# Two gaps in SBUF ahead of the experts' operands in an attention and expert-layer kernel

## The chip, the cores and the metric

The kernel runs on one core of a Trainium2 chip. The metric is the device time of one execution in microseconds (us), lower is better. TensorE is called PE, VectorE DVE, ScalarE ACT, GpSimd POOL and SyncE SP; PEld is PE's loading of the stationary operand. SBUF addresses are bytes within a partition.

## The reference

Attention over 8 batches of 8 heads: 512 local positions, each of which sees its neighbours within 32 positions and 32 global ones, and 32 global positions that see all. Its output, 4352 rows of 512 numbers, goes through an expert layer: each row goes to the one of 8 experts whose embedding is nearest in direction, and comes back weighted with the gate.

```python
xn = x / (norm(x) + 1e-6); en = emb / (norm(emb) + 1e-6)
logits = xn @ en.T / tau
e = argmax(logits); gate = softmax(logits)[e]
out[row] = gate * (relu(x[row] @ w1[e]) @ w2[e])     # w1[e]: 512 x 1024, w2[e]: 1024 x 512
```

All inputs and the output are float32.

## The kernel before

The first stage computes attention, four steps to a batch, and routes each row: its gate and number are put behind its 512 values, and an indirect DMA scatters it into a table in DRAM with a region for each expert. Two blocks of 128 rows of the first expert are computed early, in plain float32 matmuls (`early_block`, lines 157 to 184), from the raw weights in the stage tiles stg0 and stg1. Their pieces (1024 numbers and a gap of two) begin 4104 bytes apart.

The second stage runs `item(w, prev)` 36 times, in an order written out by hand. An item is 128 rows of one expert. For float32 accuracy at the matmul's single-pass type float32r, each operand is split in two: a high part, rounded to float32r, and a low part, what the rounding left. WH and WL hold the parts of the weights, four slots of 4096 numbers each: `w_part` makes them from stg, a half of an expert during each item, with a cast on ACT (L1172) and a subtraction on DVE or POOL (L1174). `x_parts` transposes the item's rows (L1154) and splits them into xH and xL (L1156, L1157); `h_parts` does that for the hidden layer (L1201, L1203, L1204) into hH and hL. `up` and `down` then make three matmuls for each product: high by high (L1178) and low weights (L1179) in `high`, and the low rows by high weights (L1183) in `low`. In all of them the part of x or h is the stationary operand, 128x128, and 512 columns of WH or WL are the moving one. From the third item on the slot of WH and WL comes from a register; in the first two it is fixed.

DMAs bring the next item's raw weights (2 MB, SP's queue) and the rows of the item after the next. The result goes out by an indirect DMA on POOL (L142).

Where a tile lies follows from the order in which the tiles are made: pools follow each other, and each tile takes its size rounded up to 32 bytes. The pools of the second stage, wp (WH, WL), xi (xr0 to xr2), xh (xH0, xH1, xL0, xL1), hb (h), ht (hL, hH) and obp (ob), lie over those of the attention stage, which are dead by then, and a tile waits for the tiles under it. In the program before, WH begins at byte 55,904 and WL at 121,440, both 96 past a multiple of 512; xH0 at 193,216 and, with steps of 2048 and 4096, the other parts, h, hL and hH begin 192 past one. The stage tiles stg0 and stg1 begin at 22,368 and 38,784, which is 352 and 384 past one.

Of the kernel before, what the change touches and what calls it, by code (L numbers as in the profile page):

```python
# [12 lines left out]
F32 = mybir.dt.float32  # L13
# [20 lines left out]
P = 128  # L34
# [65 lines left out]
def tile_kernel(ctx: ExitStack, tc: tile.TileContext, qk, va, emb, tau, wraw, cst, out):  # L100
# [30 lines left out]
    def cols(st, lo, hi):  # L131

        r = lo // WRUN
        return st[:, r, lo - r * WRUN : hi - r * WRUN]
# [886 lines left out]
    wp = ctx.enter_context(tc.tile_pool(name="wp", bufs=1, reuse_waits="tile"))  # L1021
    xi = ctx.enter_context(tc.tile_pool(name="xi", bufs=1, reuse_waits="tile"))
    xh = ctx.enter_context(tc.tile_pool(name="xh", bufs=1, reuse_waits="tile"))
# [6 lines left out]
    ps_1 = ctx.enter_context(tc.tile_pool(name="ps_1", bufs=3, space=PSUM, reuse_waits="tile"))  # L1030


    WH = wp.tile([P, 4, 4096], F32R, name="WH")
    WL = wp.tile([P, 4, 4096], F32R, name="WL")
    WH2 = WH.rearrange("p (s h) n -> p s (h n)", s=2)
    WL2 = WL.rearrange("p (s h) n -> p s (h n)", s=2)

    xrs = [xi.tile([P, ROW], F32, name=f"xr{i}") for i in range(3)]
    xHs = [xh.tile([P, 4, P], F32R, name=f"xH{i}") for i in range(2)]
    xLs = [xh.tile([P, 4, P], F32R, name=f"xL{i}") for i in range(2)]  # L1040

# [78 lines left out]
    def first_parts(hf, c):  # L1120

        cs = slice(c * 1024, (c + 1) * 1024)
        src = cols(st0[hf], cs.start, cs.stop)
        nc.scalar.copy(WH[:, hf, cs], src)
        eng = nc.gpsimd if hf == 1 and c < 2 else nc.vector
        eng.tensor_tensor(WL[:, hf, cs], src, WH[:, hf, cs], ALU.subtract)  # L1126

# [31 lines left out]
    def item(w, prev):  # L1159
# [9 lines left out]
        def w_part(c):  # L1169
            cs = slice(c * 512, (c + 1) * 512)  # L1170
            s3 = cols(st, cs.start, cs.stop).unsqueeze(1)
            made.append(nc.scalar.copy(WH[:, ds(ra, 1), cs], s3))  # L1172
            eng, r = (nc.vector, rv) if c % 2 == 1 else (nc.gpsimd, rg)
            made.append(eng.tensor_tensor(WL[:, ds(r, 1), cs], s3, WH[:, ds(r, 1), cs], ALU.subtract))  # L1174

# [204 lines left out]
```

## Time and profile before

| | us |
|---|---|
| median of 3 runs | 739.73 (738.18 to 742.41) |
| the profiled execution's own time | 740.73 |
| its span, first to last instruction | 738.9 |
| PE busy | 683.4 (92%) |
| ACT busy | 458.7 (62%) |
| DVE busy | 424.2 (57%) |

Busy matmuls overlap: the length of a matmul in the profile reaches beyond the start of the next, so its price in a stream is the step from start to start. The time outside the span is 740.73 − 738.9 = 1.8 us.

### The profile page before, as it was taken

How to read it: one execution, taken by the hardware profiler on the slowest of the kernel's cores; microseconds unless marked ns; L12 is line 12 of the kernel's file. 1: busy time of each engine (PE TensorE's matmuls, PEld its weight loads, DVE VectorE, ACT ScalarE, POOL GpSimd, SP SyncE). 2: the span in 40 equal slices, each digit the busy share in tenths (PEclk: the TensorE clock that was granted, in tenths of full speed). 3: DMA queues.
4: the chain of work that ended last, by engine and by line, in shares of the span. 5: the costliest groups of instructions: out<-in, count | busy, mean ns of one | idle time of the engine just before them, and what ended most of it. 6: DMA issues, size and time to landing. Idle time of an engine off the chain costs nothing.

```text
span 738.9 us, 23354 instructions
## 1 busy us (share of the span) xinstructions
PE 683.4 (92%) x7867; PEld 535.5 (72%) x7869; DVE 424.2 (57%) x1449; ACT 458.7 (62%) x956; POOL 274.7 (37%) x318
## 2 busy tenths in 40 slices
PE   8888878877878989999999999999999999999995
PEld 4666667655666547888888888888888888888884
DVE  2777677888677575545454555555454545554543
ACT  3776766857657265656565656566666656666653
POOL 2011122221122444544454535444444444454542
PEclk9999999999899999999999999999999999999998
DMA  9988878978997266647474656566565656565744
GB/s 276 340 234 247 274 215 270 289 212 284 281 289 219 96 219 245 247 168 257 160 255 171 231 193 225 204 202 225 192 222 180 245 177 242 174 237 178 258 155 148
DMA packets 66301, 165.14 MB, mean 223 GB/s; under 512 B 6516, under 2 KB 14580, under 8 KB 66176
## 3 DMA queue, kind: packets, MB, share of 16 engines
q1 hardware_dynamic: 60416, 145.67, 59.4%
q0 software_dynamic: 5760, 17.87, 6.8%
q8 instruction: 71, 1.16, 0.7%
q14 instruction: 54, 0.44, 0.2%
HBM read 142.49 MB, written 22.07 MB: 223 GB/s over the span
## 4 chain that ended last, share of the span: by engine, by line
PE 85%; issue 6%; DVE 4%; DMA 2%; ACT 1%; SPq 0%; POOL 0%; DVEq 0%; POOLq 0%
PE g L1183 18%; PE g L1178 18%; PE g L1179 18%; PE po L515 5%; PE pt L492 4%; PE hps L1201 4%; PE s_ps L445 4%; PE pt L632 2%; PE xps L1154 2%; DMA raw<-in_qk_dram 2%; PE po L334 2%; PE pt L600 1%; PE pt L552 1%; DVE WL L1126 1%; PE s_ps L434 1%
## 5 line engine op out<-in xcount | busy, mean ns | idle before, releaser
L1174 DVE TENSOR_TENSOR WL<-stg,WH 128x512 f32 (+1 forms) x144 | 149.6, 1039 | 125.3 <-ACT WH L1172 125.3
L1174 POOL TENSOR_TENSOR WL<-stg,WH 128x512 f32 (+1 forms) x144 | 174.1, 1209 | 90.3 <-ACT WH L1172 89.4
L1172 ACT CAST WH<-stg 128x512 f32 (+1 forms) x288 | 177.7, 619 | 4.5 <-ACT ob L140 0.5
L1178 PE MATMUL g<-WH,hH 128*128 (+1 forms) x288 | 120.0, 417 | 0.0
L1178 PE MATMUL g<-WH,xH 128*128 (+1 forms) x288 | 117.3, 407 | 0.0
L1183 PE MATMUL g<-WH,xL 128*128 (+1 forms) x288 | 114.2, 397 | 1.7 <-DVE ob L141 1.7
L1179 PE MATMUL g<-WL,xH 128*128 (+1 forms) x288 | 114.1, 396 | 0.0
L1179 PE MATMUL g<-WL,hH 128*128 (+1 forms) x288 | 113.6, 394 | 0.0
L142 POOL DMA_INDIRECT out_dram<-ob x37 | 37.3, 1009 | 154.9 <-ACT ob L140 140.8
L485 ACT ACTIVATE pb<-pb,nm 128x128 f32<-128x128 f32 x256 | 80.0, 395 | 12.3 <-DVE nm L468 12.3
L1204 DVE TENSOR_TENSOR hL<-hps,hH 128x512 fp32r<-128x512 f32 x72 | 49.8, 691 | 62.7 <-ACT hH L1203 62.7
L1183 PE MATMUL g<-WH,hL 128*128 (+1 forms) x288 | 84.6, 395 | 0.0
L1183 PEld LDWEIGHTS g<-WH,xL 128*128 128x128 f32 x288 | 54.0, 188 | 15.1 <-DVE ob L141 2.1
L1195 ACT ACTIVATE h<-g 128x512 f32<-128x512 f32 x72 | 42.8, 594 | 35.3 <-PE g L1183 35.3
L1183 PEld LDWEIGHTS g<-WH,hL 128*128 128x128 f32 x288 | 54.4, 189 | 13.1
L1178 PEld LDWEIGHTS g<-WH,xH 128*128 128x128 f32 x288 | 54.3, 189 | 11.8 <-issue 0.2
L1179 PEld LDWEIGHTS g<-WL,xH 128*128 128x128 f32 x288 | 54.4, 189 | 11.6 <-issue 0.2
L140 ACT ACTIVATE ob<-g,xr 128x512 f32<-128x512 f32 x36 | 24.8, 688 | 60.9 <-PE g L1183 60.9
L772 POOL DMA_INDIRECT xs<-xt,si x32 | 32.1, 1003 | 81.7 <-PE s_ps L445 30.4
L1179 PEld LDWEIGHTS g<-WL,hH 128*128 128x128 f32 x288 | 54.4, 189 | 9.8
L1178 PEld LDWEIGHTS g<-WH,hH 128*128 128x128 f32 x288 | 54.2, 188 | 9.7
L1203 ACT CAST hH<-hps 128x512 fp32r<-128x512 f32 x72 | 42.1, 584 | 26.4 <-PE hps L1201 26.3
(200 smaller groups left out, 991.4 us busy)
## 6 DMA issues: line engine op xcount, KB each, us to landing
stg<-in_wraw_dram SPq DMA_DIRECT2D x36, 2048.0 KB
vt<-in_va_dram SPq DMA_DIRECT2D x94, 260.0 KB
raw<-in_qk_dram SPq DMA_DIRECT2D x56, 304.0 KB
xr<-xs SPq DMA_DIRECT2D x38, 257.0 KB
stg<-in_wraw_dram SPq DMA_DIRECT2D x16, 256.0 KB
vt<-in_va_dram SPq DMA_DIRECT2D x30, 130.0 KB
xs<-fill SPq DMA_DIRECT2D x12, 257.0 KB
stg<-in_wraw_dram SPq DMA_DIRECT2D x4, 512.0 KB
```

Source lines behind the costliest of these rows:

```text
L142: nc.gpsimd.indirect_dma_start(out=out[:, :], out_offset=bass.IndirectOffsetOnAxis(ap=ob[:, DM : DM + 1].bitcast(U32), axis=0), in_=ob[:, ...
L485: nc.scalar.activation(pb[:, cs], pb[:, cs], AF.Exp, bias=nm[:, n : n + 1], scale=-1.0)
L515: ins = nc.tensor.matmul(po[32 * k : 32 * k + 32, grp, j * VH : (j + 1) * VH], pT[:, col(s, k, j) : col(s, k, j) + 32], vals(b, _window(4 ...
L772: ins = nc.gpsimd.indirect_dma_start(out=xs[:, :], out_offset=bass.IndirectOffsetOnAxis(ap=st["si"][:, t : t + 1], axis=0), in_=get(t), in ...
L1172: made.append(nc.scalar.copy(WH[:, ds(ra, 1), cs], s3))
L1174: made.append(eng.tensor_tensor(WL[:, ds(r, 1), cs], s3, WH[:, ds(r, 1), cs], ALU.subtract))
L1178: reads.append(nc.tensor.matmul(o.unsqueeze(1), a, WH2[:, ds(rp, 1), sl], start=first, stop=False))
L1179: reads.append(nc.tensor.matmul(o.unsqueeze(1), a, WL2[:, ds(rp, 1), sl], start=False, stop=False))
L1183: reads.append(nc.tensor.matmul(o.unsqueeze(1), a, WH2[:, ds(rp, 1), sl], start=False, stop=last))
L1195: nc.scalar.activation(h[:, nh * 512 : (nh + 1) * 512], g, AF.Relu)
L1203: nc.scalar.copy(hv, hp_)
L1204: nc.vector.tensor_tensor(hL[:, nh * 4 : nh * 4 + 4, :].rearrange("p c n -> p (c n)"), hp_, hv, ALU.subtract)
```

## The change

Two tiles of 104 float32 numbers, 416 bytes, are made and never used: one ahead of WH, one ahead of xH0. All that follows in the second stage's pools moves by 416 bytes, and behind the second gap by 832. WH, WL, xH, xL, h, hL and hH then begin on multiples of 512 bytes (56,320, 121,856, 194,048 and so on); the row tiles xr move from 96, 128 and 160 past a multiple to 0, 32 and 64. The attention stage's tiles and the stage tiles stay where they are.

```diff
@@ -1030,12 +1030,14 @@
     ps_1 = ctx.enter_context(tc.tile_pool(name="ps_1", bufs=3, space=PSUM, reuse_waits="tile"))
 
 
+    wp.tile([P, 104], F32, name="gap0")
     WH = wp.tile([P, 4, 4096], F32R, name="WH")
     WL = wp.tile([P, 4, 4096], F32R, name="WL")
     WH2 = WH.rearrange("p (s h) n -> p s (h n)", s=2)
     WL2 = WL.rearrange("p (s h) n -> p s (h n)", s=2)
 
     xrs = [xi.tile([P, ROW], F32, name=f"xr{i}") for i in range(3)]
+    xh.tile([P, 104], F32, name="gap1")
     xHs = [xh.tile([P, 4, P], F32R, name=f"xH{i}") for i in range(2)]
     xLs = [xh.tile([P, 4, P], F32R, name=f"xL{i}") for i in range(2)]
```

## Rows read from the trace of the kernel before

**Rows 1.** The page: busy us (share of the span) and instructions.
```profile
span 738.9 us, 23354 instructions
PE 683.4 (92%) x7867; PEld 535.5 (72%) x7869; DVE 424.2 (57%) x1449; ACT 458.7 (62%) x956; POOL 274.7 (37%) x318
```

**Rows 2.** The stretch of the items, with its columns.
```profile
core 0: us, PE busy (x) PEld busy (x) DVE busy (x) ACT busy (x) POOL busy (x), PEclk, DMA share, GB/s
...
279.50:729.70 450.20, 449.86 (x2156) 366.75 (x2157) 223.59 (x290) 282.04 (x501) 210.40 (x180) 1.00 0.60 211
```

**Rows 3.** The chain that ended last, by engine, from the page.
```profile
PE 85%; issue 6%; DVE 4%; DMA 2%; ACT 1%; SPq 0%; POOL 0%; DVEq 0%; POOLq 0%
```

**Rows 4.** The same chain in order of time: each item's last four matmuls.
```profile
291.22 0.94 PE g L1183 x4
303.75 0.94 PE g L1183 x4
...
716.98 0.94 PE g L1183 x4
```

**Rows 5.** The page's costliest groups: busy us, mean ns of one | idle before.
```profile
L1178 PE MATMUL g<-WH,hH 128*128 (+1 forms) x288 | 120.0, 417 | 0.0
...
L1183 PE MATMUL g<-WH,xL 128*128 (+1 forms) x288 | 114.2, 397 | 1.7 <-DVE ob L141 1.7
```

**Rows 6.** Timeline of PE in one item: start us, us, instruction.
```profile
504.87 0.40 PE L1178 MATMUL g<-WH,xH 128*128 x1
505.11 0.40 PE L1179 MATMUL g<-WL,xH 128*128 x1
505.34 0.39 PE L1183 MATMUL g<-WH,xL 128*128 x1
505.57 0.40 PE L1178 MATMUL g<-WH,xH 128*128 x1
...
509.09 0.60 PE L1201 MATMUL hps<-ident,h 128*128 128x128 f32 x4
...
509.76 0.39 PE L1179 MATMUL g<-WL,xH 128*128 x1
```

**Rows 7.** Timeline of PE at the start: warm-up matmuls.
```profile
9.33 2.97 PE L334 MATMUL po<-ones 128*128 128x512 bf16 x13 [0.16 <-issue]
...
14.46 2.10 PE L334 MATMUL po<-ones 128*128 128x512 bf16 x9
```

**Rows 8.** The early block's matmuls by line and form, 250 to 282 us.
```profile
L184 PE MATMUL g<-stg,hH 128*128 128x512 f32 x16 | 7.4, 592 | 0.0
L171 PE MATMUL g<-stg,hL 128*128 128x512 f32 x16 | 7.3, 598 | 0.8 <-ACT hL L164 0.8
L184 PE MATMUL po<-stg,raw 128*128 128x512 f32 x16 | 7.2, 592 | 0.0
```

**Rows 9.** Timeline of PE in the first early block.
```profile
255.13 4.46 PE L184 MATMUL po<-stg,raw 128*128 128x512 f32 x10
```

**Rows 10.** Timeline of PE in the first item.
```profile
280.18 0.40 PE L1178 MATMUL g<-WH,xH 128*128 128x512 f32 x1
...
281.82 0.40 PE L1179 MATMUL g<-WL,xH 128*128 128x512 f32 x1
```

**Rows 11.** Weight loads by line and form, 380 to 735 us.
```profile
L1183 PEld LDWEIGHTS g<-WH,xL 128*128 128x128 f32 x224 | 42.0, 188 | 10.1
L1201 PEld LDWEIGHTS hps<-ident,h 128*128 128x128 f32 x224 | 27.9, 141 | 7.5
```

**Rows 12.** The page's groups of ACT and DVE in the items.
```profile
L1174 DVE TENSOR_TENSOR WL<-stg,WH 128x512 f32 (+1 forms) x144 | 149.6, 1039 | 125.3 <-ACT WH L1172 125.3
...
L1172 ACT CAST WH<-stg 128x512 f32 (+1 forms) x288 | 177.7, 619 | 4.5 <-ACT ob L140 0.5
...
L1204 DVE TENSOR_TENSOR hL<-hps,hH 128x512 fp32r<-128x512 f32 x72 | 49.8, 691 | 62.7 <-ACT hH L1203 62.7
```

**Rows 13.** The chain between the stages.
```profile
269.46 4.29 DVE WL L1126 x2
```

## The prediction

> **What bounds the kernel now.** I read the page's busy table first. PE is busy for 92% of the span; ACT, the next one, for 62% [rows 1]. [...] The third view, the chain that ended last, says the same from the other side: it is 85% PE [rows 3], and the four matmuls that end each item come back in it at an even step, 291.22, 303.75, ... 716.98. Those are 35 items with 34 steps between them: (716.98 − 291.22) / 34 = 12.522 us for each item [rows 4]. 36 items make 450.8 us, 61% of the 738.9 us span.
>
> So in this stage nothing waits that matters; the time is the number of PE instructions times their spacing. The page counts six groups of 288 matmuls g (two of them stand in [rows 5]), 1728 in all or 48 for each item. Their mean of about 0.4 us is no price, because they overlap. The price is start to start, in the timeline: from 504.87 to 509.09 there are 18 matmuls, 4.22 / 18 = 0.2344 us each. Four transposes and the first matmul behind them take from 509.09 to 509.76, 0.67 us, so a transpose costs (0.67 − 0.234) / 4 = 0.109 us [rows 6]. The check: 48 x 0.2344 + 12 x 0.109 = 12.56 us, against 12.522 from the chain.
>
> These matmuls are slow for their 512 columns. The warm-up matmuls, bfloat16 of the same 128x512 size, give a step free of end effects from two runs of different length: (2.97 − 2.10) / (13 − 9) = 0.2175 us [rows 7]. The excess is 0.2344 − 0.2175 = 0.017 us a matmul, 1728 x 0.017 = 29 us in the kernel. The whole question of this change is whether that excess, or a part of it, comes from where the operands begin.
>
> **The change part by part.** It adds two tiles that no instruction reads or writes, so no instruction, DMA or wait is added. It only shifts addresses: WH and WL from 96 bytes past a multiple of 512 to 0, the x rows by the same 416 bytes, and xH, xL, h, hL and hH from 192 past to 0.
>
> *The matmuls' operands.* What is a different start worth? No row here shows a split matmul (float32r, at the full rate) at another start, so I bound it. The nearest rows with different starts are the early block's float32 matmuls. L171 reads the four pieces of stg0, which begin at 352, 360, 368 and 376 past a multiple of 512; L184 reads those of stg1, at 384, 392, 400 and 408. Both last 592 ns in the mean, or 598 in the one group that has a wait in it [rows 8]. Ten of them in a row take 4.46 us, (4.46 − 0.59) / 9 = 0.430 us a step [rows 9]. That is twice the warm-up's step, 2 x 0.2175 = 0.435, so they run at half its rate with no excess, at eight starts of which none is a multiple of 512. The limit of this row is that half rate: a small cost at the start could hide in the slack that it leaves. It therefore excludes a large cost for any odd start and leaves a small one open. I take 0 a matmul. The end below is the whole excess, −0.017 us; the end above is +0.0056 us, from the mean step of 0.2344 to the 0.24 that the timeline shows for its longest steps [rows 6].
>
> [...]
>
> *Registers are not the excess.* From the third item on, the matmuls take the slot of WH from a register; the first two have it fixed. In the first item the step from 280.18 to 281.82 is 1.64 / 7 = 0.234 us [rows 10], the same. Only the data's kind and the operands' places are left as reasons.
>
> *Weight loads.* A load of xH, xL, hH or hL takes 188 ns, one of h for a transpose 141 ns [rows 11]. They run beside the preceding matmul and end before its 0.234 us step does, so a load that gets faster gives nothing. One that got longer by more than 0.234 − 0.188 = 0.046 us would show. Cost 0.
>
> *ACT, DVE and POOL.* They write WH, WL and the parts at new addresses. A cast takes 619 ns, a subtraction from PSUM 691 ns, the subtraction for WL 1039 ns, much stretched beside POOL [rows 12]; in the items all of it lies behind 449.86 us of PE. If the 8 casts of an item all got dearer, ACT, busy for 282.04 of 450.20 us there [rows 2], would need another 12.5 x (1 − 0.63) = 4.7 us an item before it was the bound. Cost 0.
>
> *The change of stages.* Shifted tiles lie over other dead tiles of the attention stage: hL and hH over later copies of pT, xL and h over another pb, the output tiles over gp. If one of these were in use later than those before, the first item would wait. All were last read by the attention matmuls, which end at 242, and the first of the shifted tiles to be written, early in the second early block, comes at about 260. The chain there goes over the DVE's subtractions from 269.46 on [rows 13], whose slots 0 and 1 of WL lie over values that the same matmuls read. Cost 0; were the cover gone, it would be tenths of a microsecond, once.
>
> *DMAs.* The x rows arrive at another start, two items (25 us) ahead of their use. Cost 0.
>
> The sum is 0: 740.7 us for the profiled execution, 1.0 us above the median of the runs shown, 739.7 us, which I forecast.
>
> **The rivals.** *A, the excess is all misplacement.* For it: only these matmuls have it, and their starts are odd. Against it: [rows 8, 9]. Price: 1728 x 0.017 = 29 us, 739.7 − 29 = 711 us, with an item of 12.522 − 48 x 0.017 = 11.7 us.
>
> [...]
>
> *B, a part of it.* An operand of 2048 bytes that begins 96 past a multiple touches five blocks of 512 bytes; an aligned one touches four. If a start in a block cost something, a fifth of the excess would go, 0.0034 us or 6 us; if each step came down to the shortest, 0.23 us, it would be 1728 x 0.0044 = 7.6 us; half the excess is 15 us. I put B at 731 us, from 724 to 735. For it: a small cost at the start fits both [rows 6] and [rows 9].
>
> *C, slower.* Now the moving operand and the weights that are loaded beside it begin at the same place of a block; before they were 96 bytes apart. If the two streams met, each matmul would lose what its longest steps lose now: 1728 x 0.0056 = 10 us, 750 us. It decides as soon as a step grows by over 0.002 us (3.7 us in all, 0.5%). Against it: loads and matmuls read side by side now at no visible loss in the transposes.
>
> *D, the shift doesn't happen.* If the gaps were placed elsewhere, the starts would stay odd and the time the same. The sizes speak against it: 416 is what is missing to 512 behind 96, and the three x rows take 6240 bytes, again 96 past a multiple.
>
> **How the numbers follow.** No effect, D included: 0.55, 737 to 743 us. A: 0.13, B: 0.19, C: 0.13. A step of 0.5% is about what this kernel's runs can tell from nothing (738.2 to 742.4 without any change). Faster is A and B, 0.32; slower is C, 0.13; the same is 0.55. The range leaves out A and the upper half of C: 724 to 748 us.
>
> **What would show it.** Right: the stretch of the items stays at 450 us, the chain's step at 12.52 us and the step of the matmuls at 0.234 us; loads stay at 188 and 141 ns. A would show in a step of 0.217 us, B in one between 0.225 and 0.232 us, C in one above 0.236 us or longer loads. A first item that starts later than 279.5 us would be the change of stages. I would be wrong above all if a read at the full rate is sensitive to its start where a read at half the rate is not.

## The result and the profile after

The changed kernel takes 732.46 us in the median (730.01 to 733.12) against 740.12 us before, measured beside it (738.18 to 742.41). The ratio is 0.9889, with a 95% interval of 0.9853 to 0.9926. So it is faster, by 1.1%, and not the same, as I had held likeliest. The time lies at rival B's 731 us, but as the experiments show not for B's reason.

The page of the profile after, its span and PE's busy time, beside [rows 1]:

```profile
span 731.3 us, 23356 instructions
PE 675.7 (92%) x7869; PEld 535.3 (73%) x7869; DVE 424.6 (58%) x1449; ACT 458.9 (63%) x956; POOL 274.4 (38%) x318
```

The stretch of the items, as in [rows 2]:

```profile
core 0: us, PE busy (x) PEld busy (x) DVE busy (x) ACT busy (x) POOL busy (x), PEclk, DMA share, GB/s
...
279.38:722.05 442.67, 442.67 (x2156) 366.28 (x2157) 223.50 (x289) 282.45 (x503) 210.91 (x180) 1.00 0.61 215
```

The span is 738.9 − 731.3 = 7.6 us shorter. PE's busy time in the items fell from 449.86 to 442.67 us, by 7.19 us, for the same 2156 matmuls at the same granted clock of 1.00; ACT's, DVE's and PEld's did not move by as much as 0.5 us. All but 0.4 us of the gain is thus in PE's stream.

The chain after, each item's last four matmuls, as in [rows 4] (the two new lines move L1183 to L1185, and the others with it):

```profile
290.59 0.91 PE g L1185 x4
302.91 0.92 PE g L1185 x4
...
709.52 0.92 PE g L1185 x4
```

Its step is (709.52 − 290.59) / 34 = 12.322 us, 0.200 us less than before; 36 x 0.200 = 7.2 us, the same sum from another view. The timeline of PE after, the run of 18 matmuls that starts an item, against [rows 6]:

```profile
500.83 0.39 PE L1180 MATMUL g<-WH,xH 128*128 x1
501.06 0.39 PE L1181 MATMUL g<-WL,xH 128*128 x1
501.28 0.39 PE L1185 MATMUL g<-WH,xL 128*128 x1
501.51 0.39 PE L1180 MATMUL g<-WH,xH 128*128 x1
...
504.68 0.39 PE L1185 MATMUL g<-WH,xL 128*128 x1
504.91 0.60 PE L1203 MATMUL hps<-ident,h 128*128 128x128 f32 x4
```

18 matmuls from 500.83 to 504.91 make 4.08 / 18 = 0.2267 us each, 0.2344 before. The rest of the item gained less: 48 x 0.0077 would be 0.37 us, and it got 0.20. In the shorter runs of six and twelve matmuls behind transposes the mean step (after the first) fell only from 232.9 to 231.1 ns. What the other engines and the weight loads take is unchanged, as the page's groups after show beside [rows 11, 12]:

```profile
L1176 DVE TENSOR_TENSOR WL<-stg,WH 128x512 f32 (+1 forms) x144 | 149.8, 1040 | 124.4 <-ACT WH L1174 124.4
...
L1185 PEld LDWEIGHTS g<-WH,xL 128*128 128x128 f32 x288 | 54.1, 188 | 12.7 <-DVE ob L141 1.1
```

### The profile page after: what moved, and what is told of

The parts are those of the page before. It is cut to its first block, busy times and chain, and to the rows that moved or that the text cites. A ratio compares the mean times of both kernels' runs of the same rounds, so it can differ in the third digit from the quotient of the medians.

```text
span 731.3 us, 23356 instructions
## 1 busy us (share of the span) xinstructions
PE 675.7 (92%) x7869; PEld 535.3 (73%) x7869; DVE 424.6 (58%) x1449; ACT 458.9 (63%) x956; POOL 274.4 (38%) x318
## 4 chain that ended last, share of the span: by engine, by line
PE 83%; issue 7%; DVE 5%; DMA 3%; POOL 1%; ACT 0%; SPq 0%; POOLq 0%; DVEq 0%
PE g L1180 18%; PE g L1181 18%; PE g L1185 18%; PE po L515 5%; PE hps L1203 4%; PE pt L492 4%; PE s_ps L445 3%; PE pt L632 2%; PE xps L1156 2%; DMA raw<-in_qk_dram 2%; PE pt L552 1%; PE po L334 1%; DVE WL L1128 1%; PE pt L600 1%; PE s_ps L434 1%
## 5 line engine op out<-in xcount | busy, mean ns | idle before, releaser
L1176 DVE TENSOR_TENSOR WL<-stg,WH 128x512 f32 (+1 forms) x144 | 149.8, 1040 | 124.4 <-ACT WH L1174 124.4
L1185 PE MATMUL g<-WH,xL 128*128 (+1 forms) x288 | 112.6, 391 | 0.7 <-DVE ob L141 0.7
L1181 PE MATMUL g<-WL,xH 128*128 (+1 forms) x288 | 112.4, 390 | 0.0
L1185 PE MATMUL g<-WH,hL 128*128 (+1 forms) x288 | 83.4, 391 | 0.0
L1185 PEld LDWEIGHTS g<-WH,xL 128*128 128x128 f32 x288 | 54.1, 188 | 12.7 <-DVE ob L141 1.1
L1185 PEld LDWEIGHTS g<-WH,hL 128*128 128x128 f32 x288 | 54.1, 188 | 12.2
```

What stands on the lines that cost most here:

```text
L1181: reads.append(nc.tensor.matmul(o.unsqueeze(1), a, WL2[:, ds(rp, 1), sl], start=False, stop=False))
L1185: reads.append(nc.tensor.matmul(o.unsqueeze(1), a, WH2[:, ds(rp, 1), sl], start=False, stop=last))
```

## The experiments

All vary nothing but the two gaps, unless the text says otherwise. Theory M holds that the start of the moving operand counts, S that of the stationary one, and R the distance between the two within a block of 512 bytes; R' is R with blocks of 256. I call a kernel by the bytes past a multiple of 512 at which WH and WL, and then the parts of x and h, begin: before is 96/192, the changed kernel 0/0. A weight load is the load of a stationary operand, here a part of x or h; WH and WL are the moving ones. One number is read from each: the step from item to item in the chain, as above. The single time of a run says less, because the start of the items differs by several us between the profiled executions: the first item's last matmuls start at 283.44 us in 32/0 and at 292.96 us in 0/64, and these took 731.55 and 742.43 us with nearly the same step. The time before by itself runs from 732.93 to 742.41 us. The step comes from one profiled execution of each layout.

**0/192, WH and WL alone.** The second gap is made shorter, so that the parts stay where they were:

```diff
-    xh.tile([P, 104], F32, name="gap1")
+    xh.tile([P, 24], F32, name="gap1")
```

> Only WH and WL are put on multiples of 512; xH, xL, h, hH and hL stay 192 bytes past one. Theory M (the start of the moving operand costs): the whole gain comes, items at 12.32 us, steps in a long run of matmuls at 0.227 us, about 732 us. Theory S (the start of the stationary operand costs): nothing, items at 12.52 us and 740 us. Theory R (what counts is the distance between the two starts within a block of 512): distance 192 where before it was 96, so steps other than 0.227 us, 735 to 745 us.

Measured: ratio 0.9914 (0.9886 to 0.9943). The chain and the timeline of PE of this run:

```profile
294.29 0.92 PE g L1185 x4
...
701.44 0.92 PE g L1185 x4
```

```profile
504.78 0.39 PE L1180 MATMUL g<-WH,xH 128*128 x1
505.01 0.39 PE L1181 MATMUL g<-WL,xH 128*128 x1
505.23 0.39 PE L1185 MATMUL g<-WH,xL 128*128 x1
505.46 0.39 PE L1180 MATMUL g<-WH,xH 128*128 x1
...
508.90 0.60 PE L1203 MATMUL hps<-ident,h 128*128 128x128 f32 x4
```

Items are (701.44 − 294.29) / 33 = 12.338 us, nearly the whole gain. The long run has (508.90 − 504.78) / 18 = 0.229 us a step in place of an even 0.227. That looks like theory M with a small remainder; the 735 to 745 us that R named did not come.

**96/0, the parts alone.**

```diff
-    wp.tile([P, 104], F32, name="gap0")
...
-    xh.tile([P, 104], F32, name="gap1")
+    xh.tile([P, 80], F32, name="gap1")
```

> Only xH, xL, h, hH and hL are put on multiples of 512; WH and WL stay 96 bytes past one. Theory M: nothing, items at 12.52 us and 740 us. Theory S: the whole gain, items at 12.32 us and 732 us. Theory R: the distance is 96 with the other sign, so no run of even 0.227 us steps, 735 to 745 us.

Measured: ratio 1.0003 (0.9971 to 1.0034). The chain of this run:

```profile
286.70 0.94 PE g L1184 x4
...
711.92 0.93 PE g L1184 x4
```

Items are (711.92 − 286.70) / 34 = 12.506 us. Theory S falls, and M seems to stand.

**256/256 and 0/256.** The gaps are 160 and 416 bytes, and 416 and 160.

> All of the shifted tiles begin 256 bytes past a multiple of 512. Theory R: the distance is 0 as in the changed kernel, items at 12.32 us and 732 us. Theories M and S with blocks of 512 bytes: no gain, items near 12.5 us and 740 us; with blocks of 256 bytes or less: 12.32 us as under R.

> WH and WL on multiples of 512, the parts of x and h 256 bytes past one. Theory M: items at 12.32 us, 732 us. Theory S with blocks of 512: items at 12.52 us. Theory R: the largest distance that there is in a block of 512, so the result furthest from the changed kernel's 12.32 us, to either side.

Measured: items of (705.14 − 286.22) / 34 = 12.321 us and (706.71 − 287.90) / 34 = 12.318 us, both as in the changed kernel. Multiples of 512 are not needed, 256 does as well for either operand. R with blocks of 512 falls; with blocks of 256 it stays.

**64/0, 128/0, 32/0 and 0/64.** If the start of the moving operand in some line decides, 64/0 or at least 128/0 has to be fast, and 0/64 nearly so.

> WH and WL begin 64 bytes past a multiple of 512, the parts of x and h on one. Theory 64 (the moving operand is fetched in lines of 64 bytes, and a start inside a line costs one line more): as at 0, a steady step of 0.227 us and items at 12.32 us. Theories 128 and 256 (longer lines): as at 96, a mean step of 0.233 us and items at 12.51 us. Theory R' (the distance to the stationary operand's start counts within 256 bytes): neither of the two.

> WH and WL begin 128 bytes past a multiple of 512, the parts of x and h on one. Theories 64 and 128: a step of 0.227 us and items at 12.32 us. Theory 256: items at 12.51 us, as at 96. Theory R': neither.

> WH and WL begin 32 bytes past a multiple of 512, the parts of x and h on one. All three line theories: a mean step of 0.233 us and items at 12.51 us, as at 96, since any start inside a line costs one line. Theory R': something else than at 96.

> WH and WL on multiples of 512, the parts of x and h 64 bytes past one. At 192 bytes the stationary operand cost 0.016 us an item, at 256 nothing. If its lines are of 128 bytes: the same as at 192, items at 12.34 us and a step that alternates about 0.229 us. If they are of 64 bytes and 192 did it by the distance of the two streams: another value, or 12.32 us.

The chains of 128/0, of 0/64 and of 64/0, in three fences, and the timeline of 64/0:

```profile
289.87 0.93 PE g L1185 x4
...
714.11 0.94 PE g L1185 x4
```

```profile
292.96 0.93 PE g L1185 x4
...
718.57 0.93 PE g L1185 x4
```

```profile
288.44 0.92 PE g L1185 x4
...
708.47 0.92 PE g L1185 x4
```

```profile
499.24 0.40 PE L1180 MATMUL g<-WH,xH 128*128 x1
499.47 0.39 PE L1181 MATMUL g<-WL,xH 128*128 x1
499.70 0.39 PE L1185 MATMUL g<-WH,xL 128*128 x1
499.93 0.39 PE L1180 MATMUL g<-WH,xH 128*128 x1
...
503.36 0.60 PE L1203 MATMUL hps<-ident,h 128*128 128x128 f32 x4
```

Items are (714.11 − 289.87) / 34 = 12.478 us at 128/0, (718.57 − 292.96) / 34 = 12.518 us at 0/64, (708.47 − 288.44) / 34 = 12.354 us at 64/0 and (707.90 − 283.44) / 34 = 12.484 us at 32/0. 0/64 decides against M: WH and WL begin on a multiple of 512 and nothing is gained. No line length explains why 64/0 is fast and 128/0 slow. The distance does, counted from the start of WH to that of the parts, as the remainder after division by 256 (modulo 256): 64/0 and 0/192 are both at 192, and the long run takes (503.36 − 499.24) / 18 = 0.229 us a step here as there, in the same rhythm, 232, 226, 229 ns over and over (starts of the matmuls to the nanosecond; within 2 ns in every item).

**96/96, no operand on a multiple of anything large.** Only the second gap is kept; this tells M and R' apart in the other direction.

```diff
-    wp.tile([P, 104], F32, name="gap0")
```

> No operand begins on a multiple of 512 or even of 64: WH and WL stay 96 bytes past one, as before, and the parts of x and h begin 96 past one too, so the distance is 0. Theory R' (what counts is the distance of the two starts, modulo 256): the whole gain, a steady step of 0.227 us, items at 12.32 us, a ratio of 0.99. Theory M in any form (the moving operand's start in a line): nothing, items at 12.51 us, a ratio of 1.00. Both cannot hold.

Measured: ratio 0.9881 (0.9839 to 0.9924). The chain of this run, and its timeline:

```profile
287.41 0.91 PE g L1184 x4
...
705.36 0.91 PE g L1184 x4
```

```profile
497.18 0.39 PE L1179 MATMUL g<-WH,xH 128*128 x1
497.40 0.39 PE L1180 MATMUL g<-WL,xH 128*128 x1
497.63 0.39 PE L1184 MATMUL g<-WH,xL 128*128 x1
...
501.03 0.40 PE L1184 MATMUL g<-WH,xL 128*128 x1
501.26 0.60 PE L1202 MATMUL hps<-ident,h 128*128 128x128 f32 x4
```

Items are (705.36 − 287.41) / 34 = 12.293 us and the long run has 4.08 / 18 = 0.2267 us a step. WH and WL lie where they lay before, and the whole gain is there. M is refuted in any form, and R' predicted it.

**0/32 and 16/0, the gaps in the series.** For 16/0 WH and WL are slices of tiles that are 128 numbers wider, from the fifth number on.

> WH and WL on multiples of 512, the parts of x and h 32 bytes past one: a distance of 32, the one multiple of 32 below 256 that has not been read. Theory R' with a gain at 0 and 192 alone: a step of 0.233 us, items at 12.48 to 12.52 us. A start that beats 0.227 us a step would show here, as 12.2 us or less. Theory M: 12.32 us.

> WH and WL begin 16 bytes past a multiple of 512 (they are slices of wider tiles), the parts of x and h on one: a distance of 240, between 224 (12.48 us an item) and 0 (12.32 us). If the distance works smoothly: items at about 12.40 us. If the two streams have to be in step to the byte, or nearly: 12.48 us or more. If 16 bytes are a line's width and nothing below 32 counts: 12.32 us.

Measured: items of (716.50 − 291.80) / 34 = 12.491 us and (709.34 − 286.37) / 34 = 12.440 us. 16 bytes already cost more than half of the gain; the expectation had named about 12.40 us if the distance works smoothly and 12.48 or more if it has to be met nearly to the byte, and the result lies between. No layout has a mean step below 0.227 us.

All layouts together, by that distance. The last two columns are read to the nanosecond in the 17 steps between the matmuls of the long run: their mean over the items, and the cycle that they run through, to 1 or 2 ns. The cycle does not begin at the same place in every item.

| distance | WH/parts | item, us | mean step, ns | rhythm of the steps, ns |
|---|---|---|---|---|
| 0 | 0/0 (changed) | 12.322 | 226.7 | 227 |
| 0 | 0/256 | 12.318 | 226.7 | 227 |
| 0 | 256/256 | 12.321 | 226.7 | 227 |
| 0 | 96/96 | 12.293 | 226.7 | 227 |
| 32 | 0/32 | 12.491 | 233.4 | 235, 232 |
| 64 | 0/64 | 12.518 | 233.3 | 233 or 234; in some items 231, 236 |
| 96 | 96/192 (before) | 12.522 | 234.5 | 238, 237, 231, 234, 235, 233, 232 |
| 128 | 128/0 | 12.478 | 233.0 | 237, 229 in 22 of 35 items; in the others seven values, 228 to 241 |
| 160 | 96/0 | 12.506 | 233.3 | 237, 231, 232 |
| 192 | 0/192 | 12.338 | 228.9 | 232, 226, 229 |
| 192 | 64/0 | 12.354 | 228.9 | 232, 226, 229 |
| 224 | 32/0 | 12.484 | 233.3 | 233, 234, 231, 235 |
| 240 | 16/0 | 12.440 | 231.7 | 234, 235, 230, 227 |

**Half a weight load.** In the changed kernel, `low` uses 64 of the 128 columns of xL and hL, but for the last matmul of a sum.

```diff
         def low(o, a, col, last):
             sl = slice(col, col + 512)
-            reads.append(nc.tensor.matmul(o.unsqueeze(1), a, WH2[:, ds(rp, 1), sl], start=False, stop=last))
+            n = P if last else P // 2
+            reads.append(nc.tensor.matmul(o[:n].unsqueeze(1), a[:, :n], WH2[:, ds(rp, 1), sl], start=False, stop=last))
```

> The changed kernel, in which the low part of x and h goes into the product for the first 64 rows alone, except in the last matmul of each sum (the low part of the other 64 rows is left out). Those matmuls load 64 columns of weights in place of 128 and stream the same 512. Theory L (the loss comes from the weight load that reads beside the stream): the matmul during which such a half load runs gets shorter, from 0.227 to about 0.222 us, half of its excess over 0.2175, or the rhythm breaks; with 21 half loads an item at least 0.1 us less. Theory F (a float32r stream is that slow by itself): steps and items stay at 0.227 and 12.32 us.

The weight loads by form, the chain and the timeline of PE of this run:

```profile
L1186 PEld LDWEIGHTS g<-WH,hL 128*64 128x64 f32 x193 | 25.9, 134 | 14.2
L1186 PEld LDWEIGHTS g<-WH,xL 128*64 128x64 f32 x162 | 21.7, 134 | 6.8
...
L1186 PEld LDWEIGHTS g<-WH,xL 128*128 128x128 f32 x55 | 10.3, 188 | 2.5
```

```profile
286.82 0.92 PE g L1186 x4
...
708.36 0.92 PE g L1186 x4
```

```profile
498.80 0.39 PE L1186 MATMUL g<-WH,xL 128*64 x1
499.02 0.39 PE L1180 MATMUL g<-WH,xH 128*128 x1
499.25 0.40 PE L1181 MATMUL g<-WL,xH 128*128 x1
499.49 0.39 PE L1186 MATMUL g<-WH,xL 128*64 x1
```

The expectation's count is off: 13 loads an item are halved, not 21. They did get shorter, 134 ns against 188. But the item became longer, (708.36 − 286.82) / 34 = 12.398 us, and the even rhythm was gone: the three steps above are 0.22, 0.23 and 0.24 us, and to the nanosecond they lie between 224 and 236. Theory F, by which steps and items stay, falls; theory L falls in its size: less to load did not make the item shorter. The edit does two things at once, though: with `o[:n]` the same matmuls also write 64 of the 128 partitions of their sum. Which of the two broke the rhythm, this run does not tell.

## Why the prediction was right and wrong

*What bounds the kernel, and the sum's form.* Right. The gain is matmuls times a change in their step and little else: PE lost 7.19 us of 449.86, and the span 7.6. The other terms that I put at nothing stayed there: weight loads at 188 ns, DVE's subtraction at 1040 ns (before, 0.68 us in the mean of the 59 that have none of POOL's subtractions beside them, and 1.29 us of the other 85), the first item at 279.38 us.

*The step that failed* is the one on the matmuls' operands: "I take 0 a matmul". It measured (12.322 − 12.522) / 48 = −0.0042 us a matmul in the mean, −0.0077 in the long run, and 1728 x 0.0042 = 7.2 us in all. I took the 0 from the early block's matmuls [rows 8, 9], which run at half the rate, and that was the wrong row to go by: the trace has two records for each of them (32 at L171 for 16 matmuls of the program), 0.430 us a step from record to record, where a split matmul has one, 0.234 us a step. The stationary operands of half of them, the early block's hL and hH, move with the second gap as well, and the median of their steps is 429 or 430 ns in all thirteen layouts, in which the split matmuls' mean step goes from 227 to 234 ns. Beyond that, I asked the wrong question, what a start is worth. No row of the trace before could answer what the distance between two starts is worth, since every split matmul there has the distance 96.

*Rival B* has the time, 731 us from 724 to 735, and not the cause; that its price, and with it my range, held the measured time was luck. 0/64 touches as few blocks as 0/0 and gained nothing; 96/96 touches as many as before and gained all. *Rival C* had the right place, the moving operand and the stationary one loaded beside it, and the wrong sign: that both begin at the same place of a block is the best case, 0.2267 us a step at distance 0, not the worst. Its condition, a step over 0.236 us or longer loads, did not come: no layout has a mean step over 0.2345 us, and the changed kernel's loads stay at 188 ns. *Rival A* would have needed steps of 0.217 us. (The starts to the nanosecond put the warm-up's step at 216 ns; my 0.2175 came from rounded lengths.) *Rival D* is out with the gain.

In these runs the step of the stream follows the distance of the two operands: with the same instructions it goes from 0.2267 us at distance 0 to 0.2345 us at distance 96. Whether the stream and the loads beside it share anything, no run shows. The bfloat16 warm-up takes 216 ns for its 512 columns, but no layout reaches that with the split matmuls; the best mean stays 0.011 us above.

*What is shown and what is not.* Shown: neither operand's own start decides. 96/96 and 96/192 have WH and WL at the same place, 0/0 and 96/0 have the parts at the same place, and in each pair only the one at distance 0 has the gain. The four layouts at distance 0 have the same step in the long run, the two at 192 the same rhythm; that the distance counts modulo 256 rests on these six, for every other distance has one layout. Shown too: with 64 columns in most of the low matmuls the rhythm breaks, by the shorter load or by the narrower output. Only argued: that the matmuls' own operands do it, and not the row tiles that move with WH and WL, or h and the output tiles that move with the parts. For it speaks that the change is in the long run, where PE reads nothing else; before, the rhythm there is the same in every item, whatever the other engines do beside it. Why the distance counts modulo 256 is not shown. Open: why 192 is nearly as good as 0, and what keeps 0.227 us from the warm-up's 0.216. Open is also why 96/96 has an item 0.03 us shorter than 0/0, about 1 us in the kernel and less than the runs can tell (0.9881 against 0.9889); the difference is in the matmuls behind the transposes, where the steps lie between 0.224 and 0.236 us in both before they fall into 0.227. The identity that these transposes read stays in place, 128 past a multiple of 512, while h moves; that was not tried.

The version with one gap, 96/96, is as fast as the changed kernel by the runs and slightly ahead by the chain, with 416 bytes less.

## What to carry to other kernels

Where a stream of matmuls, each with a new stationary operand, is the bound and its step is longer than that of other matmuls with as many columns, look at where the moving operand and the stationary one that is loaded beside it begin relative to each other, not at either by itself; here the same offset modulo 256 bytes gave back 7 of 740 us for an unused tile. Compare such layouts by the step in the chain or the timeline, whose mean over the items agreed to 4 ns between 0/0, 0/256 and 256/256, and not by single times, which here move by several us with the stage before. And a row at half the rate was no bound here for one at the full rate: its step stayed at 0.43 us in layouts between which the other's went from 0.227 to 0.234 us.

## What was not expected of the hardware

The step of one and the same matmul runs through a cycle that comes back in item after item: seven values from 231 to 238 ns at distance 96, four at 224 and 240, three at 160 and 192, two at 32, one at 0. At 64 and at 128 some items run through one cycle and the rest through another, and what chooses between them is open. At distance 96 the cycle holds to 1 ns in each of 35 items, though beside it a subtraction of DVE's lasts from 0.68 us, with POOL idle, to 1.97 us, beside POOL's work. Sixteen bytes of distance were enough to go from 227 ns to a cycle of 234, 235, 230 and 227, 231.7 ns in the mean.
